# In-place transposes on VectorE with ScalarE setting out the pieces, folded maxima and earlier weight sums in an attention and gated-FFN kernel

## The chip, the core and the metric

The kernel runs on one core of a Trainium2 chip. The metric is the device time of one execution in microseconds. TensorE (PE) multiplies into eight PSUM banks; VectorE (DVE), ScalarE (ACT) and GpSimd (POOL) work on tiles in SBUF, and the first two read PSUM; SyncE (SP) issues most transfers. Each engine takes its instructions in one fixed order and waits where an operand or a buffer isn't ready.

## The reference

```python
# q, k, v: (8 batches, 8 heads, 576 positions, 64); w_in (512, 2048), w_out (2048, 512); all float32
scores = (1 / sqrt(64)) * q @ k^T
mask_local   = (rel >= 0) & (rel < 32)                  # heads 0 to 3, rel = query - key position
mask_strided = (rel >= 0) & (pos_q % 32 == pos_k % 32)  # heads 4 to 7
attn = exp(scores - max) / (sum + 1e-9), masked scores at -1e9
x = (attn @ v), heads side by side: (4608 tokens, 512)
h = x @ w_in
g = h * clip(h + 3, 0, 6) / 6
out = g @ w_out
```

## The kernel before

A batch has 512 tokens that form a tile and 64 left over; the eight leftovers form one more tile of 512 tokens. Heads are worked in pairs: two local pairs and two strided pairs a batch. A local pair is cut into six blocks of 96 queries by 64 keys, a strided one into eight blocks of 128 by 18. The pair's scores go from PSUM to a tile `e`, which is masked, lowered by the row's maximum, exponentiated, summed and divided, and then turned (transposed in 32 by 32 squares) into a tile `atloc` or `atstr`, from which TensorE multiplies with v into `x`.

The FFN keeps float32 accuracy with operands split into a high part and a low rest: each product is three matmuls of 128x512 (high-high, high-low, low-high). Batches 0, 1 and 2 are plain tiles: 16 chunks of 128 hidden columns (`ph`), a gate on each, and a second product into the banks `acc`. The other five batches and the leftovers are taken in three groups of two tiles: batches 3 and 4 (`super_tile`), 5 and 6, and 7 with the leftovers (both `fast_tile`). There each pair of tiles needs seven products instead of eight: P1 to P7, of sums of weight blocks (`combine`, kept in DRAM and read back as `wr`) and sums of tiles (`form`, kept as the operands `B_...`). They share two PSUM banks: P1, P6, P7, P4 the one (`pc`), P2, P5, P3 the other (`pa`), and each result is copied out or added before the next product goes on in its bank. The second product has its own seven in the groups of 5 and of 7 (`cP`).

A gate is a relu on ScalarE into a tile `u` and a minimum and multiply on VectorE, `u<-u,ph` or `G<-u,G` (line 739). The high part is ScalarE's (`gh`, `s0`, `sp`), the low rest GpSimd's or VectorE's.

The order on each engine is written out by a small planner. Every piece of work is announced with `op(engine, us, function, reads, writes, due)`: the engine or a choice of engines with an estimated duration for each, and a due time. The planner goes through time, gives each free engine the ready piece that is due first, and so fixes the order for all engines; semaphores follow from the tiles. The estimates set only the order. `start[b]` is a tile's planned beginning, `opens[b]` to `wanted[b]` the time in which a batch's four pairs are spread.

## Time and profile before

| | |
|---|---|
| time of three executions | median 892.06 us, 890.65 to 892.85 |
| the profiled execution | 892.36 us, span 890.6 us, TensorE clock 0.992 |
| matmuls, share of the span busy | 6962, 96% |
| VectorE, GpSimd, ScalarE busy | 78%, 64%, 49% |
| VectorE busy from 690 to 760 us, where the third group opens | 66.42 of 70 us |
| ScalarE busy from 690 to 760 us | 33.77 of 70 us |

The plain tiles run from 44 to about 357 us, the first group to about 560, the second to about 720 and the third to the end, with the edges overlapping. A wait of TensorE is idle time in front of one of its instructions, put down to the instruction that released it. Idle time of another engine costs nothing by itself. A matmul is recorded longer than the distance to the next one, since matmuls overlap.

### The profile page before, as it was taken

What the parts mean: (1) busy time and instruction counts of PE and PEld (TensorE: products, weight loads), DVE (VectorE), ACT (ScalarE), POOL (GpSimd) and SP (SyncE); (2) the same over time, 40 slices, a digit from 0 to 9 for tenths busy, and PEclk for the clock granted to TensorE, in tenths of its full rate; (3) what the DMA queues carried; (4) which work ended last, traced back from release to release, by engine and by line L of the source; (5) the groups of instructions that cost most, each with busy time, mean ns of one, the idle gap of its engine ahead of it and who ended that gap; (6) DMA issues with size and microseconds to landing.
All of it is one profiled execution on the core that took longest, in us unless ns stands there. A gap on an engine that the chain in (4) does not pass through costs nothing.

```text
span 890.6 us, 18870 instructions
## 1 busy us (share of the span) xinstructions
PE 856.6 (96%) x6962; PEld 684.3 (77%) x6962; DVE 695.2 (78%) x1183; ACT 435.6 (49%) x859; POOL 570.7 (64%) x540
## 2 busy tenths in 40 slices
PE   9889999999999999999999999999999989999996
PEld 7567778787887777778777788787888767888884
DVE  5678777666758889988788756688988999777776
ACT  3677665433355454544455453464456544443431
POOL 4578877343458788966676787355666968454653
PEclk9989999999999999999999999999999999999999
DMA  8948813776774457799999797977865569766637
GB/s 208 338 92 222 247 35 89 211 218 170 239 212 103 138 126 208 234 271 276 250 269 259 242 298 236 252 192 206 216 182 172 177 181 218 221 193 192 191 117 142
DMA packets 341739, 179.11 MB, mean 201 GB/s; under 512 B 200272, under 2 KB 321872, under 8 KB 341648
## 3 DMA queue, kind: packets, MB, share of 16 engines
q1 hardware_dynamic: 333252, 176.34, 71.0%
q10 hardware_dynamic: 8396, 1.57, 1.0%
q8 instruction: 55, 0.90, 0.4%
q14 instruction: 36, 0.29, 0.1%
HBM read 136.97 MB, written 40.89 MB: 200 GB/s over the span
## 4 chain that ended last, share of the span: by engine, by line
PE 71%; DVE 11%; POOL 7%; DMA 4%; issue 3%; ACT 2%; SPq 1%; ACTq 0%; POOLq 0%; DVEq 0%
PE P L1069 7%; PE P L1070 7%; PE P L1071 7%; PE ph L815 4%; PE cP L1391 4%; PE cP L1392 4%; PE cP L1393 4%; PE ph L816 4%; PE acc L792 4%; PE ph L817 4%; PE acc L794 3%; PE acc L793 3%; PE acc L1156 3%; PE acc L1158 3%; PE acc L1157 3%
## 5 line engine op out<-in xcount | busy, mean ns | idle before, releaser
L754 POOL TENSOR_TENSOR gl<-u,gh 128x512 fp32r<-128x512 f32 x48 | 64.4, 1343 | 47.5 <-ACT gh L750 30.2
L1069 PE MATMUL P<-B_T,wr 128*128 128x512 f32 x192 | 75.8, 395 | 2.6 <-DVE r L1077 1.4
L792 PE MATMUL acc<-wo,gh 128*128 128x512 f32 x192 | 76.9, 401 | 0.0
L1409 DVE SCALAR_TENSOR_TENSOR C<-cP,C 128x512 f32<-128x512 f32 x96 | 64.4, 679 | 15.7 <-PE cP L1393 15.2
L794 PE MATMUL acc<-wo,gl 128*128 128x512 f32 x192 | 75.5, 393 | 1.1 <-POOL gl L754 1.1
L793 PE MATMUL acc<-wo,gh 128*128 128x512 f32 x192 | 75.1, 391 | 0.0
L1070 PE MATMUL P<-B_T,wr 128*128 128x512 f32 x192 | 75.0, 390 | 0.0
L1071 PE MATMUL P<-B_T,wr 128*128 128x512 f32 x192 | 74.8, 390 | 0.0
L669 DVE STREAM_TRANSPOSE atloc<-e 32x192 f32<-32x192 f32 x168 | 61.8, 368 | 7.2 <-POOL e L648 5.2
L635 POOL TENSOR_TENSOR e<-e,st 96x384 f32<-96x384 f32 (+1 forms) x64 | 43.7, 691 | 36.7 <-DVE st L631 35.5
L666 DVE STREAM_TRANSPOSE atstr<-e 32x256 f32<-32x256 f32 x128 | 55.6, 435 | 11.3 <-POOL e L648 9.9
L1069 PE MATMUL P<-B_B,wr 128*128 128x512 f32 x144 | 57.3, 398 | 2.6 <-DVE G L1277 1.1
L648 POOL TENSOR_TENSOR e<-e,st 96x384 f32<-96x384 f32 (+1 forms) x64 | 42.8, 674 | 24.3 <-DVE st L644 17.3
L1070 PE MATMUL P<-B_B,wr 128*128 128x512 f32 x144 | 56.4, 392 | 1.3 <-POOL B_B L1005 1.3
L1071 PE MATMUL P<-B_B,wr 128*128 128x512 f32 x144 | 56.1, 390 | 0.0
L736 ACT ACTIVATE u<-ph,three 128x512 f32<-128x512 f32 x48 | 33.0, 687 | 47.2 <-PE ph L817 46.5
L815 PE MATMUL ph<-x,wi 128*128 128x512 f32 x128 | 53.6, 419 | 1.1 <-ACT x L417 0.9
L1082 DVE TENSOR_TENSOR G<-P,G 128x512 f32<-128x512 f32 x64 | 43.7, 683 | 13.9 <-PE P L1071 12.5
L816 PE MATMUL ph<-x,wi 128*128 128x512 f32 x128 | 51.4, 402 | 2.3 <-issue 1.5
L817 PE MATMUL ph<-x,wi 128*128 128x512 f32 x128 | 51.3, 401 | 0.0
L750 ACT CAST gh<-u 128x512 fp32r<-128x512 f32 x48 | 29.7, 620 | 34.4 <-DVE u L739 31.9
L1069 PEld LDWEIGHTS P<-B_T,wr 128*128 128x128 f32 x192 | 36.0, 188 | 12.5 <-ACT G L1077 1.8
(613 smaller groups left out, 2600.7 us busy)
## 6 DMA issues: line engine op xcount, KB each, us to landing
wr<-dS SPq DMA_DIRECT2D x96, 256.0 KB
wr<-dA SPq DMA_DIRECT2D x72, 256.0 KB
or<-do SPq DMA_DIRECT2D x32, 512.0 KB
or<-dT SPq DMA_DIRECT2D x32, 512.0 KB
or<-do SPq DMA_DIRECT2D x48, 256.0 KB
rawi<-in_moe_w_in_dram SPq DMA_DIRECT2D x16, 512.0 KB
rawo<-in_moe_w_out_dram SPq DMA_DIRECT2D x16, 512.0 KB
do<-wo SPq DMA_DIRECT2D x16, 512.0 KB
```

Source lines behind the costliest of these rows:

```text
L669: nc.vector.transpose(at[PAD * (a + h):PAD * (a + h) + PAD, :, rows], e[rows, :, PAD * h:PAD * h + PAD])
L754: (nc.vector if tail else nc.gpsimd).tensor_tensor(out=to, in0=src(), in1=tiles[gk[0]].bitcast(F32), op=ALU.subtract)
L792: nc.tensor.matmul(acc, gh, woh, start=fc == 0, stop=False)
L793: nc.tensor.matmul(acc, gh, wol, start=False, stop=False)
L794: nc.tensor.matmul(acc, gl, woh, start=False, stop=end)
L815: nc.tensor.matmul(ph, wih, xh, start=n_ == 0, stop=False)
L816: nc.tensor.matmul(ph, wih, xl, start=False, stop=False)
L817: nc.tensor.matmul(ph, wil, xh, start=False, stop=n_ == NCC - 1)
L1069: nc.tensor.matmul(ph, wh, xh, start=fresh and k == 0, stop=False, skip_group_check=not fresh)
L1070: nc.tensor.matmul(ph, wh, xl, start=False, stop=False, skip_group_check=not fresh)
L1071: nc.tensor.matmul(ph, wl, xh, start=False, stop=k == 1, skip_group_check=not fresh)
L1409: nc.vector.scalar_tensor_tensor(out=tiles[ck], in0=tiles[bank], scalar=1.0 / 6.0, in1=tiles[ck], op0=ALU.mult, op1=ALU.add)
```

## The change

It has these parts. For batches 2 to 7 VectorE turns the whole of `e` in place with one instruction (`flip`), and ScalarE copies the 32-row pieces to their places (`spread`, six pieces of a local head, four of a strided one); for strided heads GpSimd then writes the small constant back that the sum over a row includes (`again`). For local heads of these batches the scale is applied with the mask, the maximum is taken negated, GpSimd's subtraction is gone, and ScalarE's exponential takes the maximum off as a bias, in six instructions with one block each.

The sums of weight blocks are made by quarter and half, four of the eight in the second plain tile and four in the third, into spare tiles, and stored in halves; before, the third tile made them in the weights' own place. The third group's operands `B11` and `B21` get their own buffers where attention's were (`soon`, in part), its differences too, and may be formed as soon as their inputs are there; batch 7's attention is due 25 us earlier. The second group's first products begin 10 us earlier in the plan, among the last products of the group before, and its second chunk takes the seven in another order (`TURNED`). The relu of gates in the groups goes to the PSUM bank of the product, so that the gate reads PSUM (`through`). The copies of first products (line 1077) are ScalarE's alone. Many of the planner's estimates are other numbers.

```diff
-    opens[7], wanted[7] = start[5], start[7] - FORM
+    opens[7], wanted[7] = start[5] - 5.0, start[7] - FORM - 25.0
...
+        soft = loc and b >= 2
...
+                if soft:
+                    nc.vector.scalar_tensor_tensor(out=e_of(j), in0=ps, scalar=SCALE, in1=m, op0=ALU.mult, op1=ALU.add)
+                else:
+                    nc.vector.tensor_tensor(out=e_of(j), in0=ps, in1=m, op=ALU.add)
...
-                nc.scalar.activation(e_of(j), e_of(j), AF.Exp, scale=SCALE)
+                if not soft:
+                    nc.scalar.activation(e_of(j), e_of(j), AF.Exp, scale=SCALE)
+                    return
+                for u in range(nblk):
+                    nc.scalar.activation(e_of(j)[:, u], e_of(j)[:, u], AF.Exp, bias=st_of(j, 0)[:, u:u + 1])
...
+            if not soft:
+                op("POOL", pool, less, reads=[st], writes=[ek], due=sd + 1)
...
+            if b >= 2:
+                def flip(j=j):
+                    nc.vector.transpose(e_whole(j)[:, :, :2 * PAD if loc else PAD], e_whole(j)[:, :, :2 * PAD if loc else PAD])
+
+                def spread(j=j):
+                    at, e = tiles[akeys[j]], e_whole(j)
+                    for a in range(n // PAD):
+                        rows = slice(PAD * a, PAD * a + PAD)
+                        if not loc:
+                            nc.scalar.copy(at[rows, :, rows], e[rows])
+                            continue
+                        for h in range(2):
+                            nc.scalar.copy(at[PAD * (a + h):PAD * (a + h) + PAD, :, rows], e[rows, :, PAD * h:PAD * h + PAD])
+
+                def again(j=j):
+                    nc.gpsimd.memset(e_whole(j)[:, :, NPOS:NPOS + 1], 1.0e-9)
...
-            nc.scalar.activation(new(gp, uk, [P, TOK], F32, name), source(), AF.Relu, bias=three)
+            nc.scalar.activation(tiles[through] if through else new(gp, uk, [P, TOK], F32, name), source(), AF.Relu, bias=three)
...
+    SOON = {("B11", 0): ("at", 0), ("B11", 1): ("at", 1), ("B21", 0): ("vs",)}
...
-        at = start[b0] - 10.0
+        at = start[b0] - (10.0, 10.0 + OVER, 2010.0)[si]
+        ahead = 8.0 if si == 2 else 0.0
...
-    def copied(to, writes, pk, due):
-        def go(e):
-            t = to()
-            (nc.scalar.copy if e == "ACT" else nc.vector.tensor_copy)(t, tiles[pk])
-        op({"ACT": 0.69, "DVE": 0.7}, 0, go, reads=[pk], writes=writes, due=due)
+    def copied(to, writes, pk, due):
+        def go():
+            nc.scalar.copy(to(), tiles[pk])
+        op("ACT", 0.6, go, reads=[pk], writes=writes, due=due)
...
+    TURNED = ("P2", "P1", "P5", "P6", "P3", "P7", "P4")
...
+    for n in range(4):
+        combine(n // 2, n % 2, start[1] + 6.0 + 14.0 * n)
...
+    for n in range(4, 8):
+        combine(n // 2, n % 2, start[2] + 26.0 + 14.0 * (n - 4))
```

Since the planner sorts everything anew, the order moves on every engine. Three places carry terms of the prediction. The first is TensorE's at the end of the first plain tile, in the program's order; `ph0_12` to `ph0_15` are the last four chunks, of which the even ones use one PSUM bank and the odd ones the other. Before:

```order
L817 MATMUL ph0_12_1892<-x0_30_1011,wi33_1959 128x512
L815 MATMUL ph0_13_1899<-x0_10_932,wi31_1840 128x512
L816 MATMUL ph0_13_1899<-x0_11_933,wi31_1840 128x512
L817 MATMUL ph0_13_1899<-x0_10_932,wi31_1840 128x512
L815 MATMUL ph0_13_1899<-x0_30_1011,wi33_1959 128x512
L816 MATMUL ph0_13_1899<-x0_31_1012,wi33_1959 128x512
L817 MATMUL ph0_13_1899<-x0_30_1011,wi33_1959 128x512
L815 MATMUL ph0_14_2009<-x0_00_722,wi30_1814 128x512
```

With the change:

```order
L850 MATMUL ph0_12_1854<-x0_30_1011,wi33_1963 128x512
L848 MATMUL ph0_13_1896<-x0_30_1011,wi33_1963 128x512
L849 MATMUL ph0_13_1896<-x0_31_1012,wi33_1963 128x512
L850 MATMUL ph0_13_1896<-x0_30_1011,wi33_1963 128x512
L848 MATMUL ph0_14_2011<-x0_00_722,wi30_1817 128x512
```

Between the last matmul of chunk 12 and the first of chunk 14, which goes to the same bank, three matmuls stand now instead of six.

The second place is VectorE's queue ahead of the third group, from the second group's last second products on (`cP`, which `C` gathers); `B_...`, `soon...`, lines 1005 and 1011 before and 1058 and 1064 with the change are the forming of the third group's operands. Before:

```order
L1311 TENSOR_TENSOR sp_2_4980<-G_2_5214,sp_2_4980 128x512
L1011 TENSOR_TENSOR G_2_5214<-x7_00_6967,left0_78 128x512
L1005 TENSOR_TENSOR B_B21_1_3983<-left3_81,B_B21_1_3983 128x512
L1082 TENSOR_TENSOR G_6_6013<-P2_5_7_8166,G_6_6013 128x512
L1409 SCALAR_TENSOR_TENSOR C512_7253<-cP55_20_8134,C512_7253 128x512
L1005 TENSOR_TENSOR B_B11_1_4360<-left2_80,B_B11_1_4360 128x512
L739 SCALAR_TENSOR_TENSOR G_6_6013<-u5_7P2_8213,G_6_6013 128x512
L1409 SCALAR_TENSOR_TENSOR C513_7287<-cP55_21_8156,C513_7287 128x512
L1311 TENSOR_TENSOR s15_4P4_8242<-G_1_5015,s05_4P4_8235 128x512
L1011 TENSOR_TENSOR G_2_5214<-left1_79,G_2_5214 128x512
L1011 TENSOR_TENSOR G_1_5015<-x7_30_8115,x7_20_7385 128x512
L1409 SCALAR_TENSOR_TENSOR C502_7313<-cP15_20_7970,C502_7313 128x512
```

With the change:

```order
L1361 TENSOR_TENSOR sp_2_5042<-G_2_5408,sp_2_5042 128x512
L1134 TENSOR_TENSOR G_6_6206<-P2_5_7_8372,G_6_6206 128x512
L1459 SCALAR_TENSOR_TENSOR C512_7482<-cP55_20_8342,C512_7482 128x512
L772 SCALAR_TENSOR_TENSOR G_6_6206<-P2_5_7_8372,G_6_6206 128x512
L1459 SCALAR_TENSOR_TENSOR C513_7564<-cP55_21_8362,C513_7564 128x512
L1361 TENSOR_TENSOR s15_4P4_8439<-G_1_5196,s05_4P4_8434 128x512
L1064 TENSOR_TENSOR tq_7978<-left1_79,tq_7978 128x512
L1459 SCALAR_TENSOR_TENSOR C502_7602<-cP15_20_8208,C502_7602 128x512
L1459 SCALAR_TENSOR_TENSOR C503_7627<-cP15_21_8220,C503_7627 128x512
L1361 TENSOR_TENSOR sp_1_5003<-G_4_5827,sp_1_5003 128x512
L1134 TENSOR_TENSOR G5_722_8448<-P1_5_7_8385,G5_722_8448 128x512
L1459 SCALAR_TENSOR_TENSOR C500_7803<-cP15_20_8208,C500_7803 128x512
```

In twelve rows of the same part one operation of the forming is left where five were; the others stand earlier or with GpSimd.

The third place is TensorE's opening of the third group: `P1_7_0` is the bank of P1 and then P6 of its first chunk, and P6 may begin only when P1's result has been copied out. Before:

```order
L1069 MATMUL P1_7_0_8368<-B_B11_1_4360,wr_1_4497 128x512
L1070 MATMUL P1_7_0_8368<-B_B11_1_4360,wr_1_4497 128x512
L1071 MATMUL P1_7_0_8368<-B_B11_1_4360,wr_1_4497 128x512
L1391 MATMUL cP25_30_8381<-s05_6P2_8328,or_2_4650 128x512
L1392 MATMUL cP25_30_8381<-s15_6P2_8340,or_2_4650 128x512
L1393 MATMUL cP25_30_8381<-s05_6P2_8328,or_2_4650 128x512
L1391 MATMUL cP25_30_8381<-s05_7P2_8364,or_2_4650 128x512
L1392 MATMUL cP25_30_8381<-s15_7P2_8376,or_2_4650 128x512
L1393 MATMUL cP25_30_8381<-s05_7P2_8364,or_2_4650 128x512
L1069 MATMUL P1_7_0_8368<-B_T2_0_4440,wr_2_4314 128x512
```

With the change:

```order
L1122 MATMUL P1_7_0_8562<-soonB111_8051,wr_1_4679 128x512
L1123 MATMUL P1_7_0_8562<-soonB111_8051,wr_1_4679 128x512
L1124 MATMUL P1_7_0_8562<-soonB111_8051,wr_1_4679 128x512
L1122 MATMUL P1_7_0_8562<-B_T2_0_4643,wr_2_4451 128x512
L1123 MATMUL P1_7_0_8562<-B_T2_0_4643,wr_2_4451 128x512
```

P6 (operand `B_T2`) follows P1 (operand `soonB11`) directly, where six matmuls of the second product stood between.

More of the change, by code (lines that the diff above doesn't have):

```diff
@@ L744, in gate_ops @@
         else:
-            op("DVE", 0.75, gate, reads=[uk], writes=[pk], due=du)
+            op("DVE", 0.7 if through else 1.2, gate, reads=[through or uk], writes=[pk], due=du)
     def split_ops(gk, src, key, du, name, tail=False):
@@ L897, in old, with bkey, operand @@
         return [] if si else [HOMES[key], HOMES[key] + ("lo",)] + more
+    def bkey(si, nm, k):
+        return ("soon", nm, k) if si == 2 and (nm, k) in SOON else ("B", nm, k)
+    def operand(si, nm, k):
+        key = bkey(si, nm, k)
+        if key[0] == "B":
+            return home(key)
+        if key not in tiles:
+            tiles[key] = new(ap, SOON[nm, k], [P, 2, TOK], F32R, f"soon{nm}{k}")
+        return tiles[key]
     scratch = {}
@@ L1092, in whole @@
                 on(e).tensor_tensor(out=(u, v_)[i](), in0=t[:, 0], in1=t[:, 1], op=ALU.add)
-            op({"DVE": 1.0, "POOL": 1.3}, 0, whole, reads=[slots[i]], writes=[uk[i]] + (old(("sp", 0), 0) if not n else []), due=due)
+            op({"DVE": 1.3, "POOL": 1.45}, 0, whole, reads=[slots[i]], writes=[uk[i]] + (old(("sp", 0), 0) if not n else []), due=due)
         for m in range(4):
@@ L1098, in sums @@
                 on(e).tensor_tensor(out=o, in0=x, in1=y, op=ALU.subtract)
-            op({"DVE": 0.7, "POOL": 0.9}, 0, sums, writes=uk, due=due + 0.2 + 0.1 * m)
+            op({"DVE": 0.9, "POOL": 0.85}, 0, sums, writes=uk, due=due + 0.2 + 0.1 * m)
         for i in range(2):
```

191 lines of the change are left out of this document (99 added, 92 removed).

## The prediction

> **What bounds the kernel now.** I read the page's first and fourth parts, then the busy time by stage, then who TensorE waited for, and last the groups of instructions.
>
> ```profile
> PE 856.6 (96%) x6962; PEld 684.3 (77%) x6962; DVE 695.2 (78%) x1183; ACT 435.6 (49%) x859; POOL 570.7 (64%) x540
> PE 71%; DVE 11%; POOL 7%; DMA 4%; issue 3%; ACT 2%; SPq 1%; ACTq 0%; POOLq 0%; DVEq 0%
> ```
>
> TensorE is busy for 856.6 of 890.6 us and the change takes no matmul away, so at most the 34 us in which it stands still are to be had. The stretches of the span (TensorE, its weight loads, VectorE, ScalarE, GpSimd busy; granted clock; DMA share; GB/s) say where they lie:
>
> ```profile
> 142.00:240.00 98.00, 98.00 (x1040) 78.86 (x1039) 65.96 (x152) 40.49 (x94) 43.69 (x53) 1.00 0.72 199
> 240.00:357.00 117.00, 113.59 (x1013) 90.54 (x1012) 95.34 (x169) 58.76 (x123) 86.24 (x86) 1.00 0.60 161
> 357.00:470.00 113.00, 109.49 (x891) 88.26 (x893) 98.55 (x172) 56.65 (x118) 81.53 (x82) 1.00 0.93 256
> 470.00:560.00 90.00, 88.23 (x667) 70.86 (x662) 61.62 (x106) 42.84 (x88) 64.54 (x59) 1.00 0.88 264
> 560.00:690.00 130.00, 128.78 (x844) 104.67 (x844) 110.51 (x170) 66.96 (x129) 74.51 (x62) 1.00 0.74 202
> 690.00:760.00 70.00, 64.28 (x275) 50.67 (x274) 66.42 (x75) 33.77 (x58) 56.53 (x38) 1.00 0.72 190
> ...
> 760.00:860.00 100.00, 100.00 (x438) 81.86 (x438) 73.19 (x100) 40.57 (x65) 50.51 (x35) 1.00 0.62 188
> ```
>
> Idle TensorE time is 3.4, 3.5, 1.8, 1.2 and 5.7 us in the five stretches from 240 to 760: 15.6 us in all. The rest of the 34 lies before 142 and after the last matmul. It goes with VectorE's load: 95% busy in the worst stretch (66.42 of 70), 81% to 87% where 3.4 us are lost, 67%, 68% and 73% where little or nothing is; only the 85% from 560 to 690 come cheaper, at 1.2. The clock is full. What ended these waits, in us, times, longest:
>
> ```profile
> PE ph L815 <- DVE u L739: 2.3, 3, 1.7
> PE P L1069 <- DVE r L1077: 1.4, 1, 1.4
> PE cP L1391 <- ACT B_T L1001: 1.3, 1, 1.3
> PE P L1070 <- POOL B_B L1005: 1.3, 1, 1.3
> PE ps L590 <- DVE kplain L523: 1.2, 1, 1.2
> PE cP L1392 <- DVE sp L1311: 1.1, 1, 1.1
> PE P L1069 <- DVE u L739: 0.9, 1, 0.9
> PE cP L1391 <- issue: 0.7, 1, 0.7
> ```
>
> They are single stops of 0.7 to 1.7 us. A stop costs more than its idle time. In the stretch 760 to 860 us 438 matmuls without a gap take 100 us, 0.228 each, but one is recorded as busy for 0.39. Three stops where a PSUM bank had to be emptied first (start, duration; in brackets the idle time, where it is long enough to be listed):
>
> ```profile
> 133.34 0.39 PE L817 MATMUL ph<-x,wi 128*128 128x512 f32 x1
> ...
> 133.87 0.51 PE L815 MATMUL ph<-x,wi 128*128 128x512 f32 x1
> ...
> 567.97 0.39 PE L1071 MATMUL P<-B_B,wr 128*128 128x512 f32 x1
> 568.51 0.51 PE L1069 MATMUL P<-B_B,wr 128*128 128x512 f32 x1
> ...
> 569.79 0.39 PE L1071 MATMUL P<-B_B,wr 128*128 128x512 f32 x1
> 570.85 0.50 PE L1069 MATMUL P<-B_T,wr 128*128 128x512 f32 x1 [0.68 <-ACT G L1077]
> ```
>
> From start to start the last takes 1.06 instead of 0.228: 0.83 lost for 0.68 of idle time. I count 0.16 on top of every idle stop. It is also the price of a product that follows at once in the bank that ScalarE must still copy out. The first loses 0.53 - 0.23 = 0.30 with six matmuls (1.36) in between, so a bank held by the gate (ScalarE, then VectorE) comes free 1.67 after its last matmul. The middle one loses 0.31.
>
> **The change part by part.** *Transposes of batches 2 to 7.* 12 local and 12 strided pairs, two heads each: 24 blocks of six and 24 of four VectorE transposes become 48 whole ones, and the pieces go to ScalarE.
>
> ```profile
> L669 DVE STREAM_TRANSPOSE atloc<-e 32x192 f32<-32x192 f32 x168 | 61.8, 368 | 7.2 <-POOL e L648 5.2
> L666 DVE STREAM_TRANSPOSE atstr<-e 32x256 f32<-32x256 f32 x128 | 55.6, 435 | 11.3 <-POOL e L648 9.9
> L1077 DVE COPY G<-P 128x512 f32<-128x512 f32 x23 | 15.7, 684 | 11.0 <-PE P L1071 11.0
> L739 DVE SCALAR_TENSOR_TENSOR u<-u,ph 128x512 f32<-128x512 f32 x48 | 32.9, 685 | 15.7 <-ACT u L736 15.3
> L739 DVE SCALAR_TENSOR_TENSOR G<-u_1P,G 128x512 f32<-128x512 f32 x6 | 6.3, 1051 | 0.0
> ```
>
> Removed from VectorE: 24 x 6 x 0.368 + 24 x 4 x 0.435 = 94.7 us. Added: 256 columns at 0.435, and 384 at 0.57, carrying on the step from 192 to 256 columns (at most 0.74, two of 192): 24.1. The PSUM copies of L1077, now ScalarE's alone, take 26 x 0.68 = 17.8 more off it. A gate from PSUM costs 0.685, one with both inputs in SBUF 1.05. Together VectorE loses about 88 us and a little more, from 78% to near 68%, the level at which the stretches above show little idle time.
>
> *ScalarE.* The rows nearest to what it gains, and the GpSimd row that it relieves:
>
> ```profile
> L616 ACT COPY e<-ps 32x144 f32<-32x144 f32 x112 | 30.3, 270 | 20.5 <-PE ps L590 19.3
> L638 ACT ACTIVATE e<-e 96x384 f32<-96x384 f32 x32 | 16.8, 524 | 25.9 <-POOL e L635 25.6
> L638 ACT ACTIVATE e<-e 128x144 f32<-128x144 f32 x32 | 10.2, 325 | 12.0 <-POOL e L635 11.7
> L1077 ACT COPY G<-P 128x512 f32<-128x512 f32 x41 | 23.9, 583 | 29.0 <-PE P L1071 29.0
> L736 ACT ACTIVATE u<-ph,three 128x512 f32<-128x512 f32 x48 | 33.0, 687 | 47.2 <-PE ph L817 46.5
> L417 ACT COPY x<-pv 128x256 f32<-128x256 f32 x24 | 14.7, 640 | 8.2 <-PE pv L696 8.2
> L635 POOL TENSOR_TENSOR e<-e,st 96x384 f32<-96x384 f32 x32 | 28.2, 893 | 31.4 <-DVE st L631 31.3
> ```
>
> The exponentials give (524 - 325) / 240 = 0.83 ns per column. From the small copy (0.270 at 144) a copy of 192 columns takes 0.31 and one of 256 takes 0.36; the bounds are 0.27 and the 0.64 of L417. I take the small copy, which is the nearest in shape: blocks of 1.9 and 1.45 us, 24 x 3.35 = 80 us. The exponential in six pieces: 0.205 + 64 x 0.00083 = 0.26, and 0.10 more if a bias tensor costs what it does in L736 against L1077 (687 - 583), so 1.55 to 2.15 a head against 0.52: 25 to 39 us. Copies: 26 x 0.58 = 15. ScalarE goes from 436 to about 560 us (63%). GpSimd loses 24 x 0.89 = 21 us and gains 24 small memsets.
>
> The Trainium skill speaks against that split: ScalarE: Activation LUTs, "What ACT_TABLE_LOAD costs", gives an ACTIVATE with a bias tensor about 280 ns plus 0.833 ns per column, so six of 64 columns would be an estimated 2.0 us; the 104 ns between L736 and L1077 agree with the 93 ns that it puts on such an operand. By it ScalarE's sum ends at the upper of my two figures, and nothing else changes.
>
> *Weight sums.* Half of them move from the third plain tile into the second (142 to 240 us), the rest run earlier. The chain of waits shows them in the queue where the first group opens:
>
> ```profile
> 366.68 0.73 DVE qplain L523
> ...
> 368.35 1.30 DVE wi L968
> 369.64 1.44 DVE S L960
> ...
> 374.32 1.55 DVE wi L968
> ```
>
> With transposes and half of the sums gone, the stops there by VectorE (2.3 + 1.4 + 1.2 + 0.9 = 5.8 us of the 6.9 idle in 240 to 470) should mostly go. I take **-5.0**; bounds -6.9 and 0. In the tile before, VectorE has 32 us free. They cost nothing while that room covers them; without it a sum of 1.30 to 1.55 us ahead of a gate stops TensorE as in the tile after, 1 to 2 us in all. SyncE's stores double in number at half the size; a read of q, k or v queued behind one that waits for its sum comes later, which only the early opening of the next pairs covers (72% DMA share in that tile).
>
> *The third group's operands* get their own homes and are formed before the group opens. The order shows one of these operations on VectorE in twelve rows, where there were five. Of the 5.7 us idle there I take **-4.2**. But the first product's copy no longer has six matmuls behind it: **+0.8**, the price above.
>
> *The second group's opening* has two such adjacent products (P2 before P5, P6 before P7): 1.66 against 0.83 + 0.31 now, **+0.5**. *The end of the first plain tile:* three matmuls instead of six before the bank of chunk 12 is needed, 1.67 - 0.68 = 0.99 against 0.30, **+0.7**. *The rest of 470 to 690* keeps 2.2 us of idle time outside that opening; VectorE's relief takes **-1.0**.
>
> *Gates through PSUM* hold a bank for add, relu and gate: 0.68 + 0.69 + 0.68 and hand-overs of 0.15 each, 2.5 us. In the order the least left between the third product's end and that bank's next use, among pairs with such gates, is 3.4 us, since second products were drawn forward: nothing. If not, the 2.04 us of the order before would cost 0.5 at each of seven pairs.
>
> *New waits on ScalarE:* where a relu or a PSUM copy stands behind a block of 1.9 us. Plain tiles leave typically 17 matmuls (3.9 us) between uses of a bank, against 1.67 needed, so 2.2 to spare: hidden, except where the order is tight; **+1.5**, bounds 0 and 20 (below).
>
> Some ten stops fewer, 0.16 each: **-1.6**. Sum: -5.0 - 4.2 + 0.8 + 0.5 + 0.7 - 1.0 + 1.5 - 1.6 = -8.3. The profiled execution took 892.36 us, 0.3 above the median. **884 us**; likeliest case alone, 879 to 888.
>
> **The rivals.** *All stops go.* The 15.6 us of idle time and 13 x 0.16 vanish, less the 2.0 that the order adds: 892.4 - 15.7 = 877. For it: with VectorE at 67% the stretch from 142 to 240 us has none. Against: ScalarE takes on (80 + 25 to 39) / 6 = 17 to 20 us with each batch, in front of its relus.
>
> *The stops only move.* VectorE is freed, but every queue is issued in a written order, and its tight places are new ones; the DMA share of 0.93 from 357 to 470 us may end those waits next. Then the -5.0 and half of the -4.2 are missing: 891.
>
> *ScalarE becomes the engine that is late: slower.* One mechanism: a local head's six copies stand ahead of a relu whose PSUM bank the next product needs. It decides from 2.2 / 6 = 0.37 us a copy. At the 0.64 of L417 a block is 3.8 and overruns by 1.6; if half of the 24 local blocks stand so, 19 us: 884 + 19 = 903, and at 0.5, 884 + 9.6 = 894 even with the gains. For it: six ScalarE instructions for one. Against: the 0.27 of L616, on as many partitions.
>
> *The change doesn't do what it says:* excluded by the order on each engine.
>
> **How the numbers follow.** Likeliest case 0.65, all stops go 0.12, stops move 0.13, ScalarE late 0.10. A measurement of this kernel tells 0.3% (2.7 us) from no change: faster is under 889.4. Faster 0.65 + 0.12 = 0.77, same 0.13, slower 0.10. Range 876.5 to 891.5: it takes in the first rival, ends at the second, and leaves the third out.
>
> **What would show it.** Right: VectorE near 610 us, ScalarE 550 to 575, the idle time of TensorE between 240 and 760 under 9 us, no wait on L1077's VectorE copy or on the third group's operands over 1 us; a stop of about 1 us near 133 us and one of 0.7 idle just after the third group opens. Wrong: TensorE waits that end on ScalarE copies or relus in dozens, ScalarE small copies over 0.4 us, or VectorE still above 90% from 690 to 760.

## The result and the profile after

The changed kernel takes **883.51 us** (882.11 to 884.85, four runs); the kernel before, timed beside it on the same chip, 892.45. The ratio is 0.9898 with a 95% interval of 0.9868 to 0.9928: faster by 1.0%. The forecast was 884.0, range 876.5 to 891.5. The profiled execution took 884.25 us with a span of 882.5; before it was 892.36 and 890.6.

First the page of the changed kernel: its busy times, and the shares of its chain of waits.

```profile
PE 850.9 (96%) x6962; PEld 684.3 (78%) x6962; DVE 605.8 (69%) x961; ACT 558.1 (63%) x1246; POOL 555.3 (63%) x543
PE 79%; POOL 5%; DMA 5%; DVE 4%; issue 3%; ACT 2%; SPq 1%; ACTq 0%; DVEq 0%; POOLq 0%
```

VectorE gave up 89 us of work, ScalarE took 122 more, and VectorE's share of the chain fell from 11% to 4%. The stretches (columns as before):

```profile
142.00:240.00 98.00, 98.00 (x1007) 78.94 (x1007) 59.07 (x113) 71.71 (x196) 52.91 (x64) 1.00 0.80 231
240.00:357.00 117.00, 116.90 (x1074) 94.72 (x1070) 72.27 (x122) 89.60 (x231) 83.16 (x87) 1.00 0.61 163
357.00:470.00 113.00, 111.37 (x1005) 89.00 (x1005) 71.26 (x119) 81.95 (x197) 61.73 (x72) 1.00 0.92 252
470.00:560.00 90.00, 84.02 (x613) 67.72 (x598) 54.39 (x68) 54.39 (x130) 60.42 (x53) 0.98 0.84 238
560.00:690.00 130.00, 128.61 (x800) 104.81 (x793) 97.35 (x140) 83.15 (x174) 78.76 (x68) 1.00 0.71 201
690.00:760.00 70.00, 67.69 (x295) 54.85 (x294) 60.10 (x75) 38.41 (x64) 54.79 (x37) 1.00 0.71 197
```

From 240 to 470 us TensorE now stands idle for 1.7 us (6.9 before), from 690 to 760 for 2.3 (5.7 before). But from 470 to 560 it is 6.0, where it was 1.8, and there the clock is no longer full. VectorE is busy for 60% of that stretch, as little as in the tile from 142 to 240 that has no stop: the new ones do not come from its load. What ended TensorE's waits (in us, times, longest; waits on the program's opening left out):

```profile
PE P L1122 <- DVE G L1134: 4.9, 2, 3.3
PE ps L593 <- DVE kplain L526: 2.7, 1, 2.7
...
PE P L1122 <- ACT G L1129: 2.0, 3, 0.7
...
PE ph L848 <- DVE u L772: 1.1, 2, 0.8
PE P L1122 <- DVE u_3c L772: 1.0, 1, 1.0
```

The stop of 3.3 us, at 488 us, goes back over four engines. The timeline, one row of each (start, duration, what; in brackets the idle time before it and what ended it):

```profile
479.72 0.57 SPq L1195 DMA_DIRECT2D or<-do  x1
...
486.60 1.29 POOL L1144 TENSOR_TENSOR sp<-or 128x512 f32<-128x512 f32 x1 [6.82 <-DMA or<-do]
...
487.93 1.47 DVE L1150 TENSOR_TENSOR sp<-sp 128x256 f32<-128x256 f32 x1 [4.90 <-POOL sp L1144]
...
490.73 0.68 DVE L1134 TENSOR_TENSOR G<-P,G 128x512 f32<-128x512 f32 x1
...
491.46 0.50 PE L1122 MATMUL P<-B_B,wr 128*128 128x512 f32 x1 [3.29 <-DVE G L1134]
```

These are the sums of output weights for the second phase (`combine_out`), which are not urgent: the first read of such a sum is issued at 556.8 us. A read of the weights that are summed landed at 486.5; GpSimd waited 6.82 us for it, and VectorE's next instruction stood 4.90 us waiting for GpSimd. Behind it in VectorE's queue stood a transpose, another part of the sum, and only then the addition that empties a bank for TensorE.

The stop of 2.7 us, 13 us later, is of another kind. VectorE and GpSimd:

```profile
495.56 6.36 DVE L1160 TENSOR_TENSOR sp<-sp,sp 128x512 fp32r<-128x512 f32 x1
...
495.08 1.28 POOL L1160 TENSOR_TENSOR sp<-sp,sp 128x512 fp32r<-128x512 f32 x1
...
500.08 1.28 POOL L787 TENSOR_TENSOR gl_0e<-G,gh_0e 128x512 fp32r<-128x512 f32 x1
```

A subtraction took 6.36 us; the three others of its line on VectorE took 0.69, 1.35 and 2.55. Meanwhile GpSimd made five operations of 1.28 to 1.29 us, started 1.25 us apart (first and last shown), and VectorE's ended 0.56 us after the last of them. The transpose of k behind it, and the scores behind that, came late.

Between the two stops lies a third loss, which shows only in the granted clock (last three columns: clock, DMA share, GB/s):

```profile
493.60:496.40 2.80, 2.80 (x8) 2.12 (x8) 2.80 (x4) 2.14 (x4) 2.80 (x4) 0.50 0.31 86
```

At 0.50 a large matmul takes 0.427 us instead of 0.227. The half clock lasts 3.4 us (493.0 to 496.4) and costs about 1.7.

**Gain at equal work.** To see where time was won, take every matmul at the median start-to-start time of its kind (0.227 us for a large one), and compare the moments at which two kernels have done the same amount. The table gives the difference to the kernel before that arises in each stretch (its boundaries in the time of the kernel before; minus is gained). It is worked out from all matmul records of one execution each. The first column is the opening, in which executions with the same order differ by some us; it is no part of the argument. The small matmuls of attention stand at different places in the two orders: other prices for them shift up to 2 us between neighbouring columns from 142 to 519 us, but not the sum of these four (-1.8 for the changed kernel). Rows with the same order compare without that.

| us, profiled | to 142 | 142-240 | 240-356 | 356-469 | 469-519 | 519-677 | 677-759 | 759-859 |
|---|---|---|---|---|---|---|---|---|
| changed | -1.6 | -0.7 | -3.4 | -1.9 | **+4.2** | -0.1 | -4.7 | -0.9 |
| transposes back on VectorE | -1.6 | +4.1 | -0.9 | +3.0 | +0.9 | +1.1 | -4.8 | -0.9 |
| before, transposes alone moved | -2.0 | +6.9 | +6.7 | +5.2 | +2.8 | +6.3 | -0.1 | +0.1 |
| third group's due time late | -4.4 | -0.6 | -3.5 | -3.7 | +4.2 | -0.1 | -4.4 | -0.9 |
| read issued earlier | -3.4 | -0.6 | -3.4 | -2.2 | **-0.9** | 0.0 | -4.8 | -0.9 |
| that, and subtraction on GpSimd | -5.0 | -0.6 | -3.3 | -1.6 | -3.7 | +0.9 | -4.7 | -0.9 |

### The profile page after: what moved, and what is told of

Same layout as the page of the kernel before. It is cut to its first block, busy times and chain, and to the rows that moved or that the text cites. A ratio compares the mean times of both kernels' runs of the same rounds, so it can differ in the third digit from the quotient of the medians.

```text
span 882.5 us, 19109 instructions
## 1 busy us (share of the span) xinstructions
PE 850.9 (96%) x6962; PEld 684.3 (78%) x6962; DVE 605.8 (69%) x961; ACT 558.1 (63%) x1246; POOL 555.3 (63%) x543
## 4 chain that ended last, share of the span: by engine, by line
PE 79%; POOL 5%; DMA 5%; DVE 4%; issue 3%; ACT 2%; SPq 1%; ACTq 0%; DVEq 0%; POOLq 0%
PE P L1122 8%; PE P L1124 7%; PE P L1123 7%; PE ph L848 5%; PE acc L825 5%; PE cP L1443 5%; PE cP L1442 5%; PE cP L1441 5%; PE acc L827 5%; PE ph L849 4%; PE ph L850 4%; PE acc L826 4%; PE acc L1208 3%; PE acc L1210 3%; PE acc L1209 3%
## 5 line engine op out<-in xcount | busy, mean ns | idle before, releaser
L787 POOL TENSOR_TENSOR gl<-u,gh 128x512 fp32r<-128x512 f32 x48 | 65.6, 1368 | 56.2 <-ACT gh L783 40.8
L1129 ACT COPY G<-P 128x512 f32<-128x512 f32 x64 | 37.6, 587 | 46.5 <-PE P L1124 46.3
L658 POOL TENSOR_TENSOR e<-e,st 96x384 f32<-96x384 f32 (+1 forms) x64 | 47.1, 741 | 19.6 <-DVE st L654 19.3
L693 ACT COPY atloc<-e 32x192 f32<-32x192 f32 x144 | 50.9, 353 | 12.9 <-DVE e L683 11.4
L772 DVE SCALAR_TENSOR_TENSOR u<-u,ph 128x512 f32<-128x512 f32 x48 | 32.8, 686 | 36.3 <-ACT u L769 35.9
L1361 POOL TENSOR_TENSOR sp<-G,sp 128x512 fp32r<-128x512 f32 x26 | 36.0, 1393 | 30.0 <-ACT sp L1357 28.6
L848 PE MATMUL ph<-x,wi 128*128 128x512 f32 x128 | 52.4, 410 | 2.2 <-ACT x L419 1.1
L849 PE MATMUL ph<-x,wi 128*128 128x512 f32 x128 | 50.7, 396 | 2.3 <-DVE x L422 1.6
L1122 PE MATMUL P<-B_B,wr 128*128 128x512 f32 x120 | 48.0, 400 | 4.9 <-DVE G L1134 3.3
L850 PE MATMUL ph<-x,wi 128*128 128x512 f32 x128 | 50.7, 396 | 0.0
L1123 PE MATMUL P<-B_B,wr 128*128 128x512 f32 x120 | 46.9, 390 | 0.0
L1124 PE MATMUL P<-B_B,wr 128*128 128x512 f32 x120 | 46.8, 390 | 0.0
```

What stands on the lines that cost most here:

```text
L693: nc.scalar.copy(at[PAD * (a + h):PAD * (a + h) + PAD, :, rows], e[rows, :, PAD * h:PAD * h + PAD])
L787: (nc.vector if tail else nc.gpsimd).tensor_tensor(out=to, in0=src(), in1=tiles[gk[0]].bitcast(F32), op=ALU.subtract)
L848: nc.tensor.matmul(ph, wih, xh, start=n_ == 0, stop=False)
L849: nc.tensor.matmul(ph, wih, xl, start=False, stop=False)
L850: nc.tensor.matmul(ph, wil, xh, start=False, stop=n_ == NCC - 1)
L1122: nc.tensor.matmul(ph, wh, xh, start=fresh and k == 0, stop=False, skip_group_check=not fresh)
```

## The experiments

All kernels were compared with the kernel before on the same chip (its median was 892.16 to 892.46).

**1. Transposes alone, in the order of before.** The kernel before, batches 2 to 7: one transpose in place, the blocks by ScalarE; every instruction stays where its VectorE transposes stood.

```diff
+                there = nc.vector.transpose
+                if b >= 2:
+                    there = nc.scalar.copy
+                    nc.vector.transpose(e[:, :, :2 * PAD if loc else PAD], e[:, :, :2 * PAD if loc else PAD])
...
-                        nc.vector.transpose(at[rows, :, rows], e[rows])
+                        there(at[rows, :, rows], e[rows])
...
+                if b >= 2 and not loc:
+                    nc.gpsimd.memset(e[:, :, NPOS:NPOS + 1], 1.0e-9)
```

> The kernel before with one part of the change alone: batches 2 to 7 are turned in place by one VectorE instruction a head and set out by ScalarE's copies; every engine's order is otherwise that of before. VectorE should fall from 695 to about 625 us, ScalarE rise to about 520. Theory (VectorE's load makes the stops): TensorE's idle time from 240 to 470 us falls from 6.9 to under 3, and the time to 885 to 889. Rival (the stops only move, since the order is written for the old costs): 890 to 894. Rival (ScalarE is late): over 894.

Measured: **918.05 us**, ratio 1.0294 (1.0270 to 1.0318). VectorE fell to 625 us, and the kernel lost 26, the side of the second rival. From 240 to 470 us TensorE stood idle for 12.3 us, where the theory had under 3. ScalarE's waits in this kernel (us, times, longest):

```profile
ACT atstr L670 <- DVE e L666: 21.9, 18, 2.1
...
ACT atloc L673 <- DVE e L666: 13.6, 13, 2.4
```

ScalarE stood 35.5 us at the head of its queue waiting for the transpose, with relus and PSUM copies behind it; TensorE's waits that end on ScalarE's copies of first products went from 0.7 to 8.7 us. Where VectorE could transpose at once after its own work, ScalarE must first be handed the block. The relief alone is worth less than nothing: it needs an order in which the copies stand where their block is ready.

**2. Transposes back on VectorE, in the new order.** The changed kernel, all else kept.

```diff
-                    nc.vector.transpose(e_whole(j)[:, :, :2 * PAD if loc else PAD], e_whole(j)[:, :, :2 * PAD if loc else PAD])
+                    pass
...
-                            nc.scalar.copy(at[rows, :, rows], e[rows])
+                            nc.vector.transpose(at[rows, :, rows], e[rows])
...
-                            nc.scalar.copy(at[PAD * (a + h):PAD * (a + h) + PAD, :, rows], e[rows, :, PAD * h:PAD * h + PAD])
+                            nc.vector.transpose(at[PAD * (a + h):PAD * (a + h) + PAD, :, rows], e[rows, :, PAD * h:PAD * h + PAD])
...
-                    nc.gpsimd.memset(e_whole(j)[:, :, NPOS:NPOS + 1], 1.0e-9)
+                    pass
```

> The changed kernel with that part alone undone: VectorE makes the six or four transposes a head again, at the place in the order where ScalarE's copies stood; the order is otherwise kept. VectorE should rise from 606 to about 676 us, ScalarE fall to about 470. Theory: stops by VectorE come back, 887 to 892. Rival (the gain is that of the weight sums, the early forming and the new order): 883 to 885.

Measured: **890.94 us**, ratio 0.9986 (0.9965 to 1.0008), as the theory said. Two of its stretches:

```profile
240.00:357.00 117.00, 114.93 (x1071) 92.33 (x1070) 91.34 (x172) 66.72 (x168) 76.99 (x75) 1.00 0.62 167
357.00:470.00 113.00, 108.98 (x894) 86.99 (x893) 85.52 (x159) 61.16 (x142) 64.80 (x71) 0.98 0.88 235
```

With VectorE at 78% and 76% again TensorE's idle time there is 6.1 us instead of 1.7. So the two halves of the change need each other: the new order without the transposes' relief is worth 1.5 us (not told from nothing), the relief without the order costs 26, both gain 8.9.

**3. All spread copies twice**, in the new order: `for a in [x for x in range(n // PAD) for _ in range(2)]`.

> The changed kernel with every copy that sets out a piece made twice in a row (the second changes nothing in the result), order kept: blocks of 4.2 and 3.2 us instead of 2.1 and 1.6, ScalarE near 648 us. Theory (2 us to spare behind most relus, and most blocks stand before none): 884 to 889. Rival (ScalarE is the next engine to be late): over 893.

Measured: **949.12 us**, ratio 1.0646 (1.0623 to 1.0670). The doubled copies add 89.5 us to ScalarE and 65.6 to the kernel. The mean share of 63% had hidden that ScalarE is at 77% from 240 to 357 us in the changed kernel; here the stretch reads:

```profile
240.00:357.00 117.00, 105.57 (x975) 82.20 (x974) 59.27 (x109) 98.05 (x263) 60.70 (x72) 0.96 0.51 138
```

**4. One copy more in each block** (7 and 5 instead of 6 and 4), in the new order.

```diff
+                    rows = slice(0, PAD)
+                    nc.scalar.copy(at[rows, :, rows], e[rows, :, :PAD])
                     for a in range(n // PAD):
```

> One more small copy is made at the start of every block of spread copies of batches 2 to 7 (7 and 5 instead of 6 and 4; the first is made twice), the order is kept: 24 x 0.353 + 24 x 0.403 = 18 us more on ScalarE. Theory (room, as the prediction had it: 2.2 us to spare before a relu, a local block grows from 2.12 to 2.47 us): only the overrun of about 0.3 us in half of the 24 local blocks counts, 883.5 + 3 = 886 to 888. Rival (no room at all in the written order, every added us costs 0.75 as in the kernel with all copies doubled): 883.5 + 13.5 = 895 to 899. Between 888 and 895 the cost rises with the amount, and neither holds.

Measured: **885.71 us** (883.29 to 890.28), ratio 0.9931 (0.9906 to 0.9956): 2.2 us more than the changed kernel for 18 us more on ScalarE, a little under the theory's range, and far from the rival's. The intervals of this kernel and of the changed one overlap, so the 2.2 are hardly told from nothing. The cost is not 0.75 a us from the first on; where between one copy more and all of them twice it sets in was not tried.

**5. One exponential again.** GpSimd adds the negated maxima over 384 columns, one exponential follows; the order is kept.

```diff
-                for u in range(nblk):
-                    nc.scalar.activation(e_of(j)[:, u], e_of(j)[:, u], AF.Exp, bias=st_of(j, 0)[:, u:u + 1])
+                x = e_of(j)
+                nc.gpsimd.tensor_tensor(out=x, in0=x, in1=st_of(j, 0).unsqueeze(2).to_broadcast(x.shape), op=ALU.add)
+                nc.scalar.activation(x, x, AF.Exp)
```

> For batches 2 to 7 the local maximum is added (negated) by GpSimd again over the whole block of 384 columns, and one exponential of 384 columns follows on ScalarE, in place of six of 64 with the maximum as bias; the order on every engine is kept. ScalarE loses 24 x (1.54 - 0.52) = 24 us, GpSimd gains 24 x 0.89 = 21 us. Theory A (after the change ScalarE's queue has next to no room, as doubling its copies showed at 0.75 us a us): ScalarE's relief counts, and GpSimd's load at 55% covers its own; 876 to 882. Theory B (the order is written for the split, and the head's chain is as long as before, 0.89 + 0.52 against 1.54 plus a hand-over): no difference, 882 to 885. Rival C: GpSimd is late with the add, since its queue holds sums of 1.28 us without a gap, and the exponential behind it is late for the spread copies: 886 to 895.

Measured: **883.86 us**, ratio 0.9908 (0.9878 to 0.9939): no difference from the changed kernel, theory B. 24 us less on ScalarE and 20 more on GpSimd leave the time as it was. The 6.35 us subtraction and the stop behind it stood in this kernel too (3.42 us idle).

**6. The third group's operands due late.**

```diff
-        at = start[b0] - (10.0, 10.0 + OVER, 2010.0)[si]
-        ahead = 8.0 if si == 2 else 0.0
+        at = start[b0] - (10.0, 10.0 + OVER, 10.0)[si]
+        ahead = 0.0
```

> The third group's gate operands are formed at the group's own start again (10 us before it, no lead) instead of over the time since the second group; their own homes stay. Theory (the prediction's -4.2): VectorE is loaded again between 690 and 760 us, TensorE's idle time there goes from 2.3 to between 5 and 6 us, and the kernel takes 3 to 5 us longer than the changed one: 886.5 to 888.5. Rival (VectorE's relief by the transposes was enough): the idle time between 690 and 760 stays under 3 us, and the time is 882.5 to 885. Since the stops at 488 and 501 us lie ahead of most of the new order they should stand as they did; if they go, the time is 6 to 8 us lower in either case, and the idle time of the stretch decides.

Measured: **882.62 us**, ratio 0.9887 (0.9857 to 0.9917): the same as the changed kernel. The idle time from 690 to 760 is 2.6 us, on the rival's side, and the stretch 677 to 759 gains 4.4 as it gained 4.7. The edit moved less than it was meant to: the planner gives an idle engine whatever is ready, due or not, and about a quarter of the forming work still lies at 620 to 640 us (630 to 650 in the changed kernel). What became later shows as one stop in place of two:

```profile
704.47 0.50 PE L1123 MATMUL P<-B_T,wr 128*128 128x512 f32 x1 [2.38 <-POOL B_T L1058]
```

It loses 2.54, where the changed kernel has 0.85 and 1.74. So the due time is worth nothing; what the operands' own homes are worth was not separated.

**7. All weight sums in the third tile.**

```diff
-        late = g >= NQ // 2
+        late = True
...
-        combine(n // 2, n % 2, start[1] + 6.0 + 14.0 * n)
+        pass
...
-    for n in range(4, 8):
-        combine(n // 2, n % 2, start[2] + 26.0 + 14.0 * (n - 4))
+    for n in range(8):
+        combine(n // 2, n % 2, start[2] + 26.0 + 7.0 * n)
```

> All eight sums of the input weights are made in the third plain tile and after it, none in the second; the planner sets the whole order anew. Theory (a part of the -5.0 was the sums' move): between 240 and 470 us TensorE's idle time goes from 1.7 to 3 to 5 us, stops that end on VectorE gates or copies; 885 to 888. Rival (the transposes alone had freed VectorE enough): idle time in that stretch under 2.5 us, 882 to 885. Rival (the order written anew is worse in itself, wherever): over 888, with new stops in stretches that hold no such sum.

Measured: **928.26 us**, ratio 1.0398 (1.0365 to 1.0432): 45 us more, where 2 to 5 were expected. The first group's opening:

```profile
340.00:360.00 20.00, 15.78 (x66) 11.70 (x64) 19.25 (x24) 11.34 (x27) 17.52 (x14) 1.00 0.58 174
360.00:380.00 20.00, 4.73 (x94) 4.22 (x94) 16.10 (x26) 14.03 (x38) 17.48 (x20) 0.56 0.87 261
```

The sums that are left over crowd VectorE (19.25 of 20 us) and GpSimd (17.5) just where the attention heads of the opening stand in the same queues; the chain of waits there goes to and fro between steps of heads and sums. TensorE waits for the heads' copies and transposes in stops of up to 9.8 us, and the clock goes to 0.5. At equal work, the loss arises in that opening (52 us between 356 and 401 us of the time before), and nowhere else. So the move of the sums was worth much more than the part of 5.0 that the prediction had in mind, in this order; and since the whole order was set anew, the price of the same sums in another order stays open.

**8. The last sums of the first group due later** (16 us after their pair instead of 2).

```diff
-                combine_out(n, wos, s0 + (n + 1) * PAIR + 2.0)
+                combine_out(n, wos, s0 + (n + 1) * PAIR + (16.0 if n == 7 else 2.0))
```

> The output-weight sums of the last pair of the first group are due 16 us after that pair instead of 2; the planner sets the order anew from there on (about 470 us). Theory: the stop of 3.45 us at 488 us comes from a read (or<-do) that landed late, at 486.5: GpSimd's sum waited for it, VectorE's rest of the same sum waited for GpSimd at the head of its queue, and the gate copy behind it came late. With the sums 14 us later the transfer has landed, and both stops (488 and 501 us) and the half clock between them go: about 6.3 us of stops and 2 of clock, 876 to 879 us. Rival (queue rival): another instruction of the same kind stands at the head of VectorE's queue in its place, and 2 to 4 us of stops come back at another time: 880 to 884. Rival (VectorE's operation with two inputs in SBUF alone is at fault, not the transfer): the 3.45 us stop stays, 880 to 883.

Measured: **878.64 us**, ratio 0.9841 (0.9807 to 0.9876), inside the theory's range, but not for its reason. The sums came no later, only on other engines, and now VectorE itself waited for the transfer:

```profile
482.51 0.69 DVE L1144 TENSOR_TENSOR sp<-or 128x512 f32<-128x512 f32 x1 [5.73 <-DMA or<-do]
```

TensorE has one stop of 3.97 us there, with half the clock after it, and the subtraction that took 6.36 us takes under 0.8. The second stop is gone and the first is not. By the matmul records the stretch 469 to 519 gains about 1.6 of the median's 4.9 us; the rest is not located.

**9. The subtraction on GpSimd**: one instruction changes its engine, the order is kept.

```diff
             def lo(e, i=i):
                 t = tiles["sp", 1 + i]
+                e = "POOL" if (n, i) == (7, 1) else e
```

> The changed kernel with a single instruction moved from VectorE to GpSimd at the same place of the order: the low rest of the last output-weight sum of the first group, which took 6.36 us on VectorE while GpSimd ran without a gap. Theory (VectorE with two SBUF inputs gets no turn while GpSimd goes on): the stop of 2.7 us at 501 us, ended by VectorE's transpose of k, goes, and the time falls by 2 to 3 us to 880 to 882. Rival (VectorE waited for something else there, or the record is wrong): the stop stays, 883 to 884.

Measured: **878.72 us**, ratio 0.9852 (0.9827 to 0.9877): 4.8 us less than the changed kernel, more than expected. The stop at 501 us is gone; in its place an operand of GpSimd's is late by 1.49 us at 494. TensorE's two stops in this kernel:

```profile
487.92 0.50 PE L1122 MATMUL P<-B_B,wr 128*128 128x512 f32 x1 [1.11 <-DVE G L1134]
...
495.37 0.50 PE L1123 MATMUL P<-B_B,wr 128*128 128x512 f32 x1 [1.49 <-POOL B_B L1058]
```

The first stop, which the edit doesn't touch, is 1.11 us here and was 3.29. By the matmul records the stretch 469 to 519 gains 3.3 us, part of it there; so the price of the subtraction is read from experiment 11.

**10. The read issued earlier.** The changed kernel issues eight loads of q and k for a later pair (two entries of the written order, 2410 and 2412) ahead of the read that came late (2060); now they follow it. Only these rows of SyncE move.

```diff
-        for _, _, n, e in sorted(order):
+        order.sort()
+        at = {x[2]: x for x in order}
+        order = [y for x in order if x[2] not in (2410, 2412) for y in ((x, at[2410], at[2412]) if x[2] == 2060 else (x,))]
+        for _, _, n, e in order:
```

> SyncE issues the loads of q and of k for a later attention pair (four issues each) behind one read of the output weights, instead of ahead of it; nothing else moves on any engine. In the changed kernel this read is issued at 479.72 us, after 12 us in which SyncE issued one transfer after another without a gap, and lands at 486.5, when GpSimd has waited 6.82 us for it and VectorE's next instruction 4.90 us for GpSimd. Theory (the stop of 3.45 us at 488 us is SyncE's queue): the read is issued some 8 us earlier, GpSimd's wait falls under 1 us, the stop and the half clock behind it go: 883.5 - 3.4 - 2 = 878, or 880 if VectorE's starved operation still costs its 2.9 us. Rival (the transfers are at the DMA engines' limit, share 0.92): the read lands as late as before, 882 to 885. Rival (the loads of q and k are late next): a stop that ends on their transposes (L526) takes its place, 882 to 886.

Measured: **875.38 us**, ratio 0.9816 (0.9780 to 0.9851): 8.1 us under the changed kernel. SyncE's issue, GpSimd's wait, and the subtraction in this kernel:

```profile
473.13 0.51 SPq L1198 DMA_DIRECT2D or<-do  x1
...
479.11 1.41 POOL L1147 TENSOR_TENSOR sp<-or 128x512 f32<-128x512 f32 x1 [1.50 <-DMA or<-do]
...
488.46 6.35 DVE L1163 TENSOR_TENSOR sp<-sp,sp 128x512 fp32r<-128x512 f32 x1
```

The read goes out 6.6 us earlier (2 of which this execution was ahead by then), and the stop of 3.45 us and the half clock behind it are gone. From issue to landing the read took about 6.0 us, and 6.8 before: it landed sooner because it was issued sooner. So that stop was SyncE's queue, in which one transfer was issued after another for 12 us. Its size varies: with the read in its old place it was 3.29 us idle in the changed kernel, but 1.98, 0.85, 2.06 and 1.11 in experiments 4, 5, 6 and 9. The subtraction still takes 6.35 us, and its stop (2.62 idle) stands. The table shows 5.1 us gained between 469 and 519, as the theory had it; the other 3 of the median's 8.1 are not located (1.8 of the profiled difference lies in the opening).

**11. Both.** 9 and 10 in one kernel.

> The read of the run before is moved, and the starved subtraction (the low half of the last pair's second sum) is given to GpSimd, both in one kernel; all other instructions keep their place. Theory: both stops of 470 to 560 us were causes of their own, and their prices add: no stop over 1 us from 470 to 560 us but for GpSimd's own operand (1.65 us at 494 in the kernel with only the subtraction moved), 875 to 878. Rival (one price): moving either already frees the queue, and both together give what the subtraction alone gave, 878 to 880.

Measured: **874.28 us** (871.84 to 874.76), ratio 0.9787 (0.9759 to 0.9816), the lowest median here. No stop over 0.8 us is left from 430 to 550 us, and the clock is full:

```profile
470.00:560.00 90.00, 88.70 (x642) 71.32 (x641) 51.04 (x72) 61.75 (x147) 66.13 (x61) 1.00 0.87 251
```

In the stretch 469 to 519 the second price, 2.8 us, comes on top of the first (+4.2, -0.9, -3.7), but by the medians both together are only 1.1 us ahead of the read alone, and the intervals overlap.

**12. The disputed wait by itself.** Behind the last work of the changed kernel, GpSimd makes one subtraction, VectorE then one instruction on its result, while GpSimd goes on with 0, 3, 6 or 9 more.

```diff
...
+            nc.gpsimd.tensor_tensor(out=x[:, 0], in0=y[:, 0], in1=y[:, 1], op=ALU.subtract)
...
+                nc.vector.tensor_tensor(out=x[:, 2].bitcast(F32R), in0=x[:, 0], in1=x[:, 1], op=ALU.subtract)
...
+            for _ in range(many):
+                nc.gpsimd.tensor_tensor(out=z, in0=y[:, 0], in1=y[:, 1], op=ALU.subtract)
```

> The changed kernel with a measurement appended behind its last work, where no other engine is busy: twelve times, GpSimd makes one 128x512 subtraction from SBUF, VectorE then makes one instruction that reads its result, while GpSimd goes on with 0, 3, 6 or 9 more subtractions (128x512, two inputs in SBUF, 1.25 us each) without a gap. VectorE's instruction is a subtraction with both inputs in SBUF (as the one of 6.36 us), a gate with both inputs in SBUF, an addition with one input in PSUM, or a transpose of 96x384. Theory (VectorE's two-input SBUF operation is kept from SBUF until GpSimd's run ends): the subtraction takes about 0.7 to 1.1 us alone, and the length of the run and half a us with 3, 6 and 9 behind it (about 4, 8 and 11 us), while the PSUM addition and the transpose keep their 0.7 and 0.6 us. Rival (it only runs at half speed beside GpSimd): 1.3 to 2.7 us with 3, 6 and 9 alike; then the 6.36 us have another cause. The kernel's time is 60 to 90 us above the changed one's and says nothing else.

Measured (VectorE's subtraction with 0, with 6 and with 9 behind it; the addition from PSUM and the transpose with 6):

```profile
878.64 0.69 DVE L1566 TENSOR_TENSOR px<-px 128x512 fp32r<-128x512 f32 x1 [4.19 <-POOL px L1564]
...
886.16 1.73 DVE L1566 TENSOR_TENSOR px<-px 128x512 fp32r<-128x512 f32 x1 [3.71 <-POOL px L1564]
895.62 1.73 DVE L1566 TENSOR_TENSOR px<-px 128x512 fp32r<-128x512 f32 x1 [7.73 <-POOL px L1564]
...
918.58 0.69 DVE L1570 TENSOR_TENSOR px<-pps,px 128x512 f32<-128x512 f32 x1 [7.73 <-POOL px L1564]
927.72 0.57 DVE L1572 STREAM_TRANSPOSE px<-px 96x384 f32<-96x384 f32 x1 [8.45 <-POOL px L1564]
```

Half of the theory holds. It is the kind: two inputs in SBUF (the gate with both inputs there takes 1.73 too), and neither the PSUM addition nor the transpose. It is not the length: 1.73 with 3, 6 and 9 alike, the rival's number. But it is no half speed either: VectorE's operation ends 0.55 us after GpSimd's first instruction, so it waits for that one to end and then runs.

Why VectorE waited through five in the changed kernel stays open. Here GpSimd's instructions, which write one tile, start 1.34 us apart and leave 0.08 between them; in the kernels with 6.34 to 6.36 us they start 1.25 apart and leave none. But a missing gap alone is not the reason. In the changed kernel itself VectorE mostly gets in after the first instruction of such a run. One case, GpSimd's rows first:

```profile
523.77 1.63 POOL L1064 TENSOR_TENSOR G<-x,x 128x512 f32<-128x512 f32 x1
525.36 1.74 POOL L787 TENSOR_TENSOR gl_7e<-G,gh_7e 128x512 fp32r<-128x512 f32 x1
...
524.16 1.78 DVE L1058 TENSOR_TENSOR B_B<-x,B_B 128x512 fp32r<-128x512 f32 x1
```

GpSimd leaves no gap, yet VectorE's subtraction ends 0.54 us after the first of its two instructions, and the second takes 1.74 us, where the same line took 1.28 beside the 6.36.

## Why the prediction was right, and where it was not

The total was met, 8.1 us by the profile against 8.3 in the sum, and the mechanism is the one that was forecast for 240 to 470 us; but that the numbers agree so closely is in part luck. From 469 to 677 us, where the sum had -0.5, the kernel lost 4.1. What made up for it is a term of +1.5 that cost nothing, 1.3 us more than forecast in the third group, and gains where the sum had none: 0.7 from 142 to 240, 0.9 from 759 to 859, and 1.6 in the opening, which differs from one execution to the next and where the sum had +0.7. (The -1.6 for fewer stops belongs to no single stretch, and about 1 us is lost again behind 859 us.)

- **-5.0, the stops from 240 to 470.** Idle time went from 6.9 to 1.7, and 5.3 us were gained at equal work (3.2 to 6.9 with other prices for the small matmuls). With the transposes back on VectorE these stretches are 7.4 us worse than in the changed kernel (experiment 2). Right, and as far as the transposes go for the reason given; the share of the earlier weight sums is not known (experiment 7). What the sentence lacked is the condition: in the old order the same relief costs 26.
- **-4.2 + 0.8, the third group.** Idle time fell by 3.4, as the two terms say; 4.7 us at equal work. The added stop is there to the hundredth:

```profile
702.66 0.40 PE L1124 MATMUL P<-soonB,wr 128*128 128x512 f32 x1
703.73 0.50 PE L1122 MATMUL P<-B_T,wr 128*128 128x512 f32 x1 [0.68 <-ACT G L1129]
```

  1.07 from start to start, 0.84 lost. But the cause named for the -4.2 is not shown: with the due time late, and with the transposes back, the stretch gains as much. What remains of the change there (own homes, gates through PSUM, all PSUM copies on ScalarE, the order) was not taken apart. The largest stop left there, 1.58 us idle at 712, ends on a VectorE addition.
- **+0.5 and +0.7, adjacent products and the end of the first tile.** Two stops of 0.837 and 0.836 at 566 and 572 us (1.66 forecast), and one of 0.98 at 131 us (0.99 forecast):

```profile
131.10 0.39 PE L850 MATMUL ph<-x,wi 128*128 128x512 f32 x1
132.31 0.50 PE L848 MATMUL ph<-x,wi 128*128 128x512 f32 x1 [0.82 <-DVE u L772]
```

- **-1.0, the rest of 470 to 690.** This step failed. It took the stops there for VectorE's load, and load was no longer the matter: idle time rose from 3.0 to 7.4 us, and half a clock came on top. In its place stand a read behind SyncE's queue (experiment 10) and a subtraction kept from SBUF (9 and 12). Both have forerunners in the trace of before. Its chain of waits passes through a late `or<-do` at 433 and at 492 us, and two VectorE operations of that kind had taken 2.62 us at 448 and 3.19 at 489:

```profile
433.41 6.22 DMA or<-do
...
492.32 6.63 DMA or<-do
...
448.36 2.62 DVE L1108 TENSOR_TENSOR sp<-sp,sp 128x512 fp32r<-128x512 f32 x1 [1.42 <-ACT sp L1104]
...
489.13 3.19 DVE L1005 TENSOR_TENSOR B_B<-x,B_B 128x512 fp32r<-128x512 f32 x1
```

  The Trainium skill, SBUF — State Buffer, "Who interferes with whom", says that a VectorE instruction with two SBUF inputs and a GpSimd instruction that reads SBUF exclude each other, the first to issue keeping the other out. Experiment 12 agrees (0.69 alone, 1.73 beside). A prediction that looked for VectorE's two-input operations beside GpSimd's runs would have had a reason to doubt the term.
- **Gates through PSUM, put at nothing.** One stop of 0.63 us idle, at 426 us, ends on such a gate, which stood behind a VectorE sum of 1.18 us; it cost 0.79.
- **+1.5, new waits on ScalarE.** Nothing: the waits of TensorE that end on ScalarE from 130 us on are the three adjacent products (2.0 us in all), which have terms of their own. The groups:

```profile
L693 ACT COPY atloc<-e 32x192 f32<-32x192 f32 x144 | 50.9, 353 | 12.9 <-DVE e L683 11.4
L690 ACT COPY atstr<-e 32x256 f32<-32x256 f32 x96 | 38.7, 403 | 3.8 <-DVE e L683 2.9
...
L648 ACT ACTIVATE e<-e,st 96x64 f32<-96x64 f32 x144 | 36.9, 343 | 7.3 <-DVE st L637 7.3
```

  The copies took 0.353 and 0.403 us where 0.31 and 0.36 were taken, near the end of the bounds that was chosen. A local block of 2.12 us stays inside the 2.2 that the prediction had to spare, and one copy more (2.47) costs at most a few us in all (2.2 by the medians). The claim of room was right, though close.
- **The exponential in pieces**: 36.9 / 24 = 1.54 us a head, the lower end of 1.55 to 2.15. One piece is recorded with 0.343, and six in a row overlap. The prediction read the Trainium skill, ScalarE: Activation LUTs, "What ACT_TABLE_LOAD costs", only in part: the same section says that ACTIVATEs back to back overlap by about 93 ns, which would bring its estimated 2.0 us to 1.54. The trace agrees with the two taken together.
- **-1.6, fewer stops.** From 130 us on the kernel before had 18 stops that cost over 0.3 us, the changed one has 10: 8 x 0.16 = 1.3. Right within its size.
- **Rivals.** "ScalarE is late" was priced too low: at 0.64 us a copy it was to give 903, and with every copy made twice (0.71 a piece) the kernel takes 949. That run loads the strided blocks too, which the price left out; how the rest of the difference is made up was not taken apart. "The stops only move" was half of what came: they moved into 470 to 520 us. "All stops go", 877, did not come by itself; with the two causes repaired the kernel takes 874 to 875.
- **What would show it**: VectorE 605.8 (near 610) and ScalarE 558.1 (550 to 575) were right; so were the stops of 0.98 us at 131 and of 0.68 idle where the third group opens, and no wait of over 1 us ends on the third group's operands. Idle time of TensorE from 240 to 760 under 9 us was wrong, 11.4, by the two stops alone. One sign of being wrong came, small copies over 0.4 us (0.403 for the strided pieces), but not the waits on ScalarE that it stood for.

## What to carry to other kernels

When an engine is relieved, ask which instructions stand at the head of its queue for work that is not urgent: after the relief the stops came from a late read and a blocked subtraction of such sums, and moving eight loads behind one read was, by the medians, worth about as much as the whole change (8.1 and 8.9 us). A move of work to another engine and the order in which it is issued are one change: each half alone gave nothing or lost 26 us. The average share of an engine says little on the room it has; a small dose (one more copy a block) and a large one (all of them twice) measure it.

## What the runs showed of the hardware that was not expected

- A VectorE subtraction with both inputs in SBUF took 6.34 to 6.36 us in six kernels (the changed one and experiments 4, 5, 6, 10 and 12), beside a run of GpSimd operations started 1.25 us apart, and ended about half a us after its last. The Trainium skill (SBUF — State Buffer, "Who interferes with whom") has the exclusion for one instruction; that it can last over five is shown here, and not what decides between one and five.
- Half the TensorE clock follows some short stops and not others, for 3.4 us, or 6.8 in experiments 4, 5 and 8. After 3.29 us idle it came in the changed kernel, after 2.04 in experiment 2, and after 1.11 and 1.49 us, 7 us apart, in experiment 9:

```profile
498.00:500.00 2.00, 2.00 (x20) 1.16 (x19) 0.00 (x0) 1.44 (x3) 1.04 (x1) 0.50 0.97 297
```

  After 2.69 us in the changed kernel and 2.62 in experiment 10 it did not. What decides was not settled.
- SyncE issued one transfer after another, mostly in about 0.5 us each and some in 1 to 2, for 12 us ahead of the late read: its queue, not the DMA engines alone, set when that read began.
